# Attention and gated convolution on one core: tables moved among the first steps, routing moved ahead, convolution started later, one broadcast transfer for two, reciprocals of the last pair by PE transposes, more PSUM banks at both ends

## The chip, the core and the metric

The kernel runs on one core of a Trainium2 chip. The metric is the device time of one execution in microseconds (us). Runs of one kernel agree within about 2%. A run more than 1.5% above the fastest of its kernel counts as slow. Ratios and intervals below use fast runs alone; the medians quoted are over all runs. Engines in the profile: PE is TensorE (matrix multiply), PEld its weight loads, DVE is VectorE, ACT is ScalarE, POOL is GpSimd, SP issues most of the transfers (DMA).

## The reference

```python
# attention: B=4, H=8, S=768, D=64, 16 centroids per head
q_assign = argmax(einsum('bhsd,hcd->bhsc', q_n, c_n))      # k_assign likewise
mask     = q_assign[..., :, None] == k_assign[..., None, :]
attn     = softmax(where(mask, q @ k.T / 8, -1e9))
x        = (attn @ v), heads joined to 512 columns
# gated long convolution
x1, x2, x3 = split(x @ w_proj)
y   = x1 * irfft(rfft(x2) * rfft(filter_fft)) * x3
out = y @ w_out
```

## The kernel before

The work goes through 8 groups of four heads (two per batch). A group has 12 attention steps: two pairs of heads, six key blocks each. A step multiplies scores for the next key block, takes their exponent on ACT, multiplies by v ("value matmuls") and adds up the row sums on DVE. Between the matmuls of a step, units of other work are emitted so that PE has something to do: **routing** of the next group (transposes of q and k, similarity to the centroids, a one-hot of the best centroid, whose rows go by DMA into the operands of the scores), and the **convolution** of the batch before, done with matmuls against tables of sines and cosines. PE executes in the order in which the program emits. So does every other engine in its own order, which a scheduler chooses.

```python
def bank():                                   # the PSUM bank of a unit: two take turns
    return psF.tile([128, 512], F32, name="pf")

def routing(n):                               # a generator; each yield ends a unit
    ...                                       # 8 units of transposes, 2 of similarity
    nc.vector.tensor_tensor(oh, cf, m2..., op=Alu.is_equal)          # one-hot, on DVE
    for _ in range(3):
        yield                                 # three empty units
    for t in range(NT):
        nc.tensor.transpose(oT[:, t*128:(t+1)*128], ohf[...], identb) # PE waits for oh here
    nc.vector.tensor_scalar(ohT, oT[:, :S], mka, mkb, ...)
    ...                                       # 8 DMAs of one-hot rows into the score operands

def finish(self):                             # divide a pair's output by its row sums
    ...                                       # sums by 4 matmuls -> den
    nc.sync.dma_start(dd, den[0:128:32])      # through DRAM into another shape ...
    nc.sync.dma_start(dn, dd...)
    nc.vector.reciprocal(dn, dn)
    nc.sync.dma_start(dr..., dn)              # ... and back
    for hp in range(2):                       # broadcast: one row to 64 partitions, twice
        nc.sync.dma_start(rb[64*hp:64*hp+64], dr[hp:hp+1].to_broadcast([64, S]))
    nc.vector.scalar_tensor_tensor(xf, self.osb[:, :S], ..., rb, op0=Alu.add, op1=Alu.mult)
    ...                                       # sums and differences uT, copy xT

# the loop over 96 steps (w = step within the group)
if w == 0:
    for f in fill: drain(f[0])                # what is left of the convolution, in one lump
    fill = [[routing(n + 1), 17, 17], ...]    # routing spread over the twelve steps
if w == 3 and second batch or later:          # convolution of the batch before
    fill.append([hyena(b), 21, 21])
```

Before the loop the kernel routes group 0 and builds all tables; after it, the last pair is finished and the last convolution runs alone.

The softmax here doesn't subtract the row's maximum and nothing guards it: scores larger than these inputs give would overflow.

## Time and profile before

571.07 us (two runs, 568.28 and 573.85). From its profile:

| stage | us from the start |
|---|---|
| first scores / first value matmuls | 53.8 / 56.7 |
| groups 1, 2, 4, 6, 7 start | 93.3, 131.4, 261.1, 392.1, 482.7 |
| last value matmuls end; last convolution; end | 508; 520.7 to 571.7 |

A group "starts" where its first value matmuls start in the trace. Groups 2 and 3, and 4 and 5, are one full period (a batch of attention, one convolution).

The head of the page: busy time of PE, then PE's busy tenths and its granted clock in 40 equal slices.

```profile
span 571.7 us, 6805 instructions
PE 432.3 (76%) x2405; PEld 179.9 (31%) x2417; DVE 339.7 (59%) x459; ACT 257.6 (45%) x432; POOL 177.1 (31%) x168
PE   5015997987689669977689768969689778965675
PEclk9657999989699899989699899998799897996998
```

PE is the busiest engine, with holes, and the clock dips near the holes. The period of groups 4 and 5 in the window view (stretch, its length, busy us of each engine with instruction counts, granted clock, share of the DMA engines, GB/s):

```profile
261.10:392.10 131.00, 105.68 (x593) 43.68 (x592) 79.15 (x104) 61.92 (x105) 43.26 (x30) 0.92 0.24 64
```

PE is busy 105.68 of 131.00 us. What ended its idle time in the period from 130.6 to 259.8 (engine and its work, what it waited for, us in total, times, longest):

```profile
PE pf L391 <- DVE uT L379: 8.0, 1, 8.0
PE ps L325 <- DMA aug_137<-ohT: 3.7, 1, 3.7
PE ps L325 <- DMA aug_145<-ohT: 2.4, 1, 2.4
PE pf L447 <- POOL hy L437: 2.2, 1, 2.2
```

The first line is the convolution's first unit waiting for the last pair of the batch to be finished; the next two are scores waiting for one-hot rows.

```profile
DMA packets 160, 0.39 MB, mean 98 GB/s; under 512 B 32, under 2 KB 32, under 8 KB 160
rb<-dr SPq DMA_DIRECT2D x2, 192.0 KB
```

### The profile page before, as it was taken

What the parts mean: (1) busy time and instruction counts of PE and PEld (TensorE: products, weight loads), DVE (VectorE), ACT (ScalarE), POOL (GpSimd) and SP (SyncE); (2) the same over time, 40 slices, a digit from 0 to 9 for tenths busy, and PEclk for the clock granted to TensorE, in tenths of its full rate; (3) what the DMA queues carried; (4) which work ended last, traced back from release to release, by engine and by line L of the source; (5) the groups of instructions that cost most, each with busy time, mean ns of one, the idle gap of its engine ahead of it and who ended that gap; (6) DMA issues with size and microseconds to landing.
All of it is one profiled execution on the core that took longest, in us unless ns stands there. A gap on an engine that the chain in (4) does not pass through costs nothing.

```text
span 571.7 us, 6805 instructions
## 1 busy us (share of the span) xinstructions
PE 432.3 (76%) x2405; PEld 179.9 (31%) x2417; DVE 339.7 (59%) x459; ACT 257.6 (45%) x432; POOL 177.1 (31%) x168
## 2 busy tenths in 40 slices
PE   5015997987689669977689768969689778965675
PEld 3012433323234224423234224324233233322331
DVE  2907886986369534796269533696368631872630
ACT  4131766746344327746344326736354324742122
POOL 9400704405060133425060233516251221000621
PEclk9657999989699899989699899998799897996998
DMA  8970405315010205315011115312000002010002
GB/s 207 227 165 6 112 20 135 85 42 141 28 29 29 60 10 166 85 43 141 28 29 30 31 39 163 88 37 63 28 1 29 15 1 112 29 31 28 1 1 110
DMA packets 67538, 37.48 MB, mean 66 GB/s; under 512 B 56944, under 2 KB 62640, under 8 KB 67504
## 3 DMA queue, kind: packets, MB, share of 16 engines
q1 hardware_dynamic: 66304, 34.91, 22.4%
q0 software_dynamic: 1056, 2.10, 2.0%
q8 instruction: 19, 0.31, 0.2%
q14 instruction: 15, 0.12, 0.1%
q10 hardware_dynamic: 144, 0.03, 0.0%
HBM read 31.06 MB, written 6.49 MB: 66 GB/s over the span
## 4 chain that ended last, share of the span: by engine, by line
PE 45%; DVE 25%; DMA 10%; issue 8%; SPq 5%; ACT 5%; POOL 2%; POOLq 0%; DVEq 0%; ACTq 0%
PE o L340 15%; PE ps L325 8%; PE pf L391 5%; PE pf L447 4%; DMA rb<-dr 4%; PE pf L412 3%; DVE tm L401 3%; SPq L308 3%; PE pf L262 2%; PE pf L275 2%; PE pf L359 2%; DMA dr<-dn 2%; PE pf L428 2%; DVE uT L380 2%; DMA fhi<-in_moe_filter_fft_dram 1%
## 5 line engine op out<-in xcount | busy, mean ns | idle before, releaser
L329 ACT ACTIVATE p_160<-ps 128x768 f32<-128x768 f32 x32 | 26.0, 812 | 76.1 <-PE ps L325 71.0
L412 PE MATMUL pf<-xT,wpj 128*128 128x384 bf16 x256 | 50.7, 326 | 12.7 <-ACT od L431 5.7
L340 PE MATMUL o<-p_165,vraw 128*64 128x385 f32 (+1 forms) x128 | 55.0, 558 | 0.0
L340 PE MATMUL o<-p_164,vraw 128*64 128x385 f32 (+1 forms) x128 | 55.0, 558 | 0.0
L391 PE MATMUL pf<-wpj,uT 128*128 128x512 bf16 x92 | 30.4, 476 | 32.4 <-DVE uT L379 32.1
L340 PE MATMUL o<-p_161,vraw 128*64 128x385 f32 (+1 forms) x128 | 48.2, 499 | 0.0
L340 PE MATMUL o<-p_163,vraw 128*64 128x385 f32 (+1 forms) x128 | 48.2, 499 | 0.0
L340 PE MATMUL o<-p_160,vraw 128*64 128x385 f32 (+1 forms) x128 | 48.2, 499 | 0.0
L340 PE MATMUL o<-p_162,vraw 128*64 128x385 f32 (+1 forms) x128 | 48.2, 499 | 0.0
L404 POOL TENSOR_TENSOR hy<-tm 128x512 bf16<-128x512 f32 x24 | 32.1, 1360 | 50.1 <-DVE tm L401 50.1
L401 DVE TENSOR_TENSOR tm<-pf,hm 128x512 f32<-128x512 f32 x48 | 30.0, 682 | 18.4 <-PE pf L240 11.3
L329 ACT ACTIVATE p_164<-ps 128x768 f32<-128x768 f32 x32 | 26.0, 812 | 31.9 <-PE ps L325 31.9
L412 PEld LDWEIGHTS <-wpj 128*128 128x128 bf16 x256 | 23.6, 97 | 40.6 <-issue 21.1
L447 PE MATMUL pf<-wout,hy 128*128 128x512 bf16 x92 | 26.4, 438 | 11.4 <-POOL hy L437 8.8
L393 ACT CAST hy<-pf 128x512 bf16<-128x512 f32 x24 | 14.1, 586 | 44.8 <-PE pf L391 44.7
L262 PE MATMUL pf<-ident,qkraw 128*128 128x128 f32 x192 | 33.0, 286 | 1.0 <-ACT qkT L264 0.8
L264 ACT COPY qkT<-pf 128x384 f32<-128x384 f32 x64 | 30.9, 486 | 4.8 <-PE pf L262 4.8
L329 ACT ACTIVATE p_162<-ps 128x768 f32<-128x768 f32 x32 | 26.2, 818 | 14.1 <-PE ps L325 14.1
L262 PEld LDWEIGHTS pf<-ident,qkraw 128*128 128x128 f32 x192 | 25.4, 147 | 8.3 <-ACT qkT L264 2.8
L428 PE MATMUL pf<-inv,hy 128*128 128x384 bf16 (+1 forms) x128 | 22.0, 326 | 7.2 <-DVE x_1550 L417 0.6
L329 ACT ACTIVATE p_163<-ps 128x768 f32<-128x768 f32 x32 | 26.4, 824 | 1.8 <-PE ps L325 1.4
L329 ACT ACTIVATE p_161<-ps 128x768 f32<-128x768 f32 x32 | 26.1, 816 | 0.6 <-PE ps L325 0.2
(477 smaller groups left out, 951.9 us busy)
## 6 DMA issues: line engine op xcount, KB each, us to landing
qkraw<-in_q_dram SPq DMA_DIRECT2D x32, 192.0 KB
qkraw<-in_k_dram SPq DMA_DIRECT2D x32, 192.0 KB
vraw<-in_v_dram SPq DMA_DIRECT2D x8, 768.0 KB
rb<-dr SPq DMA_DIRECT2D x32, 192.0 KB
out_dram<-tm SPq DMA_DIRECT2D x12, 512.0 KB
wpj<-in_moe_w_proj_dram POOLq DMA_DIRECT2D x1, 1536.0 KB, 11.7
flo<-in_moe_filter_fft_dram SPq DMA_DIRECT2D x2, 384.0 KB
fhi<-in_moe_filter_fft_dram SPq DMA_DIRECT2D x2, 384.0 KB
```

The source lines that it names most:

```text
L262: nc.tensor.transpose(tps[:, ts(t, 128)], qr[:, 3 * ch + t].rearrange("p h d -> p (h d)"), ident)
L264: nc.scalar.copy(qkT[z][:, ch], tps[:, :384])
L308: nc.sync.dma_start(augs[aset][pr][hp][j][64 - 16 * hp:80 - 16 * hp], ohT[r0:r0 + 16])
L325: nc.tensor.matmul(sps[:, ch, :384], self.aug[hp][1][:K, ts(sk, 128)], self.aug[hp][0][:K, ts(ch, 384)], start=True, stop=True)
L329: nc.scalar.activation(p[:, :S].rearrange("p (a b) -> p a b", a=2), sps[:, :, :384], Act.Exp, scale=0.125)
L340: nc.tensor.matmul(self.o[64 * hp:64 * hp + 64, ch, :384 + ch], vv[:, 2 * self.pr + hp, sk * D:(sk + 1) * D], pb[hp][sk][:, 384 * ch:384 * ...
L391: nc.tensor.matmul(ps, uvf[:, e, kt, ts(m, 128)], wpj[:, kt, DM:2 * DM], start=(kt == 0), stop=(kt == ND - 1))
L401: nc.vector.tensor_tensor(tm[r][:, cs], ps, hm[:, i, 2 * r + cs], op=Alu.mult)
L404: nc.gpsimd.tensor_tensor(y[:, i, r], tm[r][:, 0], tm[r][:, 1], op=Alu.add)
L412: nc.tensor.matmul(ps[:, :384], wpj[:, kt, off + dt * 128:off + dt * 128 + 128], xT[:, kt, ts(ch, 384)], start=(kt == 0), stop=(kt == ND - 1))
L428: nc.tensor.matmul((pe, po)[e][:, :384], y[lo:hi, i, cs, ts(dt, 128)], inv[lo:hi, row], start=(n == 0), stop=(n == 3))
L447: nc.tensor.matmul(ps, y2[:, kt, ts(2 * tt + e, 128)], wout[:, kt], start=(kt == 0), stop=(kt == ND - 1))
```

## The change

The intent: start attention earlier by building the tables among its first steps; let routing end by step 7, so that one-hot rows are there when the next group needs them; start the convolution two steps later and spread it over both groups instead of draining it; in the last pair replace the DRAM trip by PE transposes, hidden by eight convolution units; let the units at both ends (the first routing, the last convolution) use the banks of the scores too. The core of the diff (layout changes, load order and renamed buffers cut):

```diff
 def bank():
-    return psF.tile([128, 512], F32, name="pf")
+    if spare:
+        return spare.pop(0)
+    if more_banks[0]:                          # at both ends only
+        more_banks[0] += 1
+        if more_banks[0] % 4 in (0, 2):
+            w = psS.tile([128, 2, 512], F32, name="ps")
+            spare.append(w[:, 1])              # the two halves of one tile
+            return w[:, 0]
+    return psF.tile([128, 512], F32, name="pf")[:]
 ...
 def finish(self):
-    for hp in range(2):
-        nc.sync.dma_start(rb[64 * hp:64 * hp + 64], dr[hp:hp + 1].to_broadcast([64, S]))
+    nc.sync.dma_start(rb, dr[:].unsqueeze(1).to_broadcast([2, 64, S]))
+def finish_on_pe(self):                        # last pair: transposes, no DRAM
+    ...
 def hyena(b, xT, uT, last=False):
+    if last:                                   # gates early, then all inversions
+        gates(0); convolve(); gates(1..3); invert(0..3)
 ...
 def emit(nf):
-    (take from the list that is furthest behind)
+    for f in fill:                             # first list with something left
+        if f[1] > 0: f[1] -= 1; next(f[0], None); break
 ...
 if w == 0:
-    for f in fill: drain(f[0])
-    fill.append([routing(n + 1), NR, NR])
+    if n == 0: fill.append([tables(), NTAB, 12])
+    fill.append([routing(n + 1), NR, 7])
+    if hq: fill.append([hq, rest of its units, 12])
-if w == 3 and ...:
+if w == 5 and ...:
     (start the convolution)
```

## The prediction

> **What bounds the kernel now.** TensorE and its waits. The page gives PE 432 of 572 us busy (DVE 340, ACT 258). In the timeline a bare attention step repeats every 2.20 us with PE nearly full, and takes 2.86 with two routing units (2.20 + 2 x 0.33): steps are PE-bound. The chain of waits and PE's wait table show the rest:
>
> - Start: first scores at 53.8 us. PE waits 13.7 us for the one-hot and 14.5 for the filter sum, whose load ends at 44.7; then tables run alone.
> - Each batch period (130.6 to 259.8, three times): 8.0 us for uT at the first convolution unit, 3.7 and 2.4 for one-hot rows at group ends, some 10 of short waits, mostly where the convolution's rest is drained in one lump (196.5 to 219, two banks). After the long waits matmuls take 0.85 instead of 0.49 us, costing about 7 us more; the clock row dips there. The Trainium skill ("TensorE: Matmul & The Clock Gate", "HAM oscillation") warns of PE-idle gaps over about 3.4 us; the trace agrees. About 97 of 129 us is work.
> - End: last values near 510; PE idle 10.7 us until 520.7 (reciprocals through DRAM), then 51 us of the last convolution, with about 14 us of PE waits.
>
> **What changes, stage by stage.**
> 1. Tables move into group 0's first steps. Before first scores some 6.3 MB must load (q, k, v of two groups, filter): at the 210 to 225 GB/s of the window table, about 29 us; the one-hot chain on DVE shares it with sine work and filter sums. First scores near 39 us (34 to 44). The first steps give back 6 to 9 us: about 10 us of DVE evacuations (0.75 each). Group 0 ends at 80 instead of 91: 11 us gained.
> 2. Routing in steps 0 to 6: one-hot rows land before the group ends; 6 us of waits and 4 of slow clock per batch go. Convolution starts later, so the 8 us wait falls below 1.5, with its 2.6 us of slow clock. No lump: about 6 us of its waits hide behind attention. Added: dense steps of five units waiting for evacuations. A batch takes 104 us instead of 129. Group 1 gains 4, two batches 50; group 6 takes 52 instead of 91, as half its convolution moves into group 7: 39.
> 3. The last group now carries units: 26.4 + 1.3 + about 10 + waits = 41 instead of 30: 11 lost. Eight remaining units hide the reciprocals: 9 us instead of 10.7.
> 4. Six banks in the last convolution, gates early, adds and products split between DVE and POOL: PE work about 30 us, then last products and store: 40 instead of 51.
>
> Stage ends: 80, 116, 220, 324, 376, 417, 426, 466. I shade it to 470.
>
> **Predicted: 470 us**, 80% range 452 to 490. Faster by over 2%: 0.96; within: 0.02; slower: 0.02.
>
> **What would show it.** (1) First scores at 34 to 44; first three steps 4 to 5.5 us each. (2) Waits for one-hot rows gone from PE's table, uT waits under 5 us in total, batch period 100 to 108, granted clock in the middle at least 0.96 (now 0.90 to 0.97), PE busy 84 to 88%. (3) Last group about 41 us, no DRAM reciprocals at the end. (4) First projection to end about 40.
>
> **What would make it wrong.** Filter loads ahead of k, or filter sums ahead of the one-hot chain on DVE, delaying first scores past 45. Fill units stalling in-order PE on DVE or ACT evacuations, since DVE goes to about 75% busy: a batch near 112, giving 490. The uT chain slowed by q and k loads on the same queue. Less stall than I charge: 452.

## More of the kernel before

The broadcast of the reciprocals, which will matter: first the chain that ended last (start, us, what), then the DMA view of the 4 us around it, then what DVE waited for at the instructions that read rb (us, times).

```profile
140.49 1.50 DMA dr<-dn
142.55 3.29 DMA rb<-dr
145.96 1.03 DVE x_1165 L377
```

```profile
DMA rb<-dr: 28.2, 9
```

128 packets carry the rows (3072 bytes each). The 32 packets under 512 B are of 4 bytes, 16 for each of the two transfers. I read them as completion marks, one from each DMA engine that took part.

## The result, and the profile after

**650.44 us** (two runs, 651.56 and 649.32), 13.9% slower: the ratio is 1.139, 95% interval 1.114 to 1.164. (A ratio is the mean time of one kernel's fast runs over that of the other's in the same rounds, so it is not quite the ratio of the medians quoted.) I had expected 470.

The head of the page after, with the shares of the chain that ended last:

```profile
span 649.7 us, 6805 instructions
PE 455.3 (70%) x2426; PEld 184.8 (28%) x2426; DVE 341.5 (53%) x474; ACT 259.3 (40%) x430; POOL 151.4 (23%) x154
PE   1538899089249587779785885789667688958565
PEclk9959899689759697799999798889879699779798
PE 42%; DMA 23%; DVE 19%; issue 6%; ACT 6%; POOL 1%; SPq 1%; DVEq 0%; ACTq 0%; POOLq 0%
DMA rb<-dr 19%; PE o L347 15%; PE ps L332 7%; PE pf L460 5%; PE pf L499 3%; DMA dr<-dn 2%; PE pf L366 2%; PE pf L478 2%; DVE tm L447 2%; DMA vraw<-in_v_dram 1%; PE ps L460 1%; PE pf L436 1%; POOL hy L487 1%; DVE uT L420 1%; ACT qkT L273 1%
```

The costliest item of the chain is now a transfer of 384 KB, 19% of it; as two transfers it was 4% before. One landing in the chain, the DMA view of the ten us around it, and DVE's wait in total:

```profile
250.08 9.36 DMA rb<-dr
```

```profile
DMA packets 130, 0.39 MB, mean 39 GB/s; under 512 B 2, under 2 KB 2, under 8 KB 130
rb<-dr SPq DMA_DIRECT2D x1, 384.0 KB
```

```profile
DMA rb<-dr: 107.7, 15
```

The same 128 data packets, but two completion packets instead of 32: two DMA engines carried it. A second view agrees. The busy tenths of the 16 DMA engines, in 40 slices of the same two windows, before and after, stay at 1 while the one transfer runs (two of 16 engines are 12.5%), and reach 8 and 9 for the two:

```profile
DMA  0000000000466974877787876211000000000000
DMA  0000001011111111111111111111111111110000
```

In the chains it takes 9.4 to 12.5 us instead of 3.3 to 5.6. The Trainium skill states the rule in "DMA: Bandwidth & Descriptors", section "Rules for kernel authors": an outermost dimension of size c below 16, such as a leading broadcast, confines the DMA to at most c engines. The source here is walked as 2 x 64 x 768, and the trace agrees: two.

DVE executes in order, and what stands behind the read of rb waits too. The timeline of DVE at that landing (start, us, instruction, and in brackets the idle time before it and what ended it; two lines of uT are left out before the last):

```profile
252.57 0.96 DVE L304 TENSOR_TENSOR oh<-cand,m_1724 128x768 bf16<-128x768 bf16 x1
259.53 1.02 DVE L387 SCALAR_TENSOR_TENSOR x_1636<-osb,rb 128x768 f32<-128x768 f32 x1 [6.01 <-DMA rb<-dr]
260.47 0.67 DVE L312 TENSOR_SCALAR ohT<-pf,mka,mkb 128x768 bf16<-128x768 bf16 x1
262.31 0.95 DVE L354 TENSOR_TENSOR acc_1643<-acc_1643,p_144 128x768 f32<-128x768 f32 x1
```

Routing's evacuation (ohT) and the row sums (acc) stand behind data that they do not use: PE had finished the input of ohT at 254.4, and ohT starts at 260.47. In PE's waits this shows under other names:

```profile
PE pf L310 <- DVE oh L304: 64.8, 7, 20.9
PE pf L249 <- DVE tm L447: 19.8, 3, 9.8
```

The waits of the kernel before are gone: none for uT, and one of 5.5 us for one-hot rows, at the very start. The period of groups 4 and 5 runs from 308.9 to 454.6, 145.7 us, instead of 131.

### The profile page after: what moved, and what is told of

Read it like the earlier page. It is cut to its first block, busy times and chain, and to the rows that moved or that the text cites. A ratio compares the mean times of both kernels' runs of the same rounds, so it can differ in the third digit from the quotient of the medians.

```text
span 649.7 us, 6805 instructions
## 1 busy us (share of the span) xinstructions
PE 455.3 (70%) x2426; PEld 184.8 (28%) x2426; DVE 341.5 (53%) x474; ACT 259.3 (40%) x430; POOL 151.4 (23%) x154
## 3 DMA queue, kind: packets, MB, share of 16 engines
q10 hardware_dynamic: 3968, 2.36, 1.5%
## 4 chain that ended last, share of the span: by engine, by line
PE 42%; DMA 23%; DVE 19%; issue 6%; ACT 6%; POOL 1%; SPq 1%; DVEq 0%; ACTq 0%; POOLq 0%
DMA rb<-dr 19%; PE o L347 15%; PE ps L332 7%; PE pf L460 5%; PE pf L499 3%; DMA dr<-dn 2%; PE pf L366 2%; PE pf L478 2%; DVE tm L447 2%; DMA vraw<-in_v_dram 1%; PE ps L460 1%; PE pf L436 1%; POOL hy L487 1%; DVE uT L420 1%; ACT qkT L273 1%
## 5 line engine op out<-in xcount | busy, mean ns | idle before, releaser
L347 PE MATMUL o<-p_141,vraw 128*64 128x385 f32 (+1 forms) x128 | 58.1, 584 | 0.0
L347 PE MATMUL o<-p_142,vraw 128*64 128x385 f32 (+1 forms) x128 | 58.1, 584 | 0.0
L336 ACT ACTIVATE p_144<-ps 128x768 f32<-128x768 f32 x32 | 26.3, 822 | 76.7 <-PE ps L332 75.9
L460 PE MATMUL pf<-xT,wpj 128*128 128x384 bf16 x212 | 46.4, 351 | 9.8 <-DVE tm L447 6.6
L347 PE MATMUL o<-p_146,vraw 128*64 128x385 f32 (+1 forms) x128 | 52.1, 533 | 0.0
L347 PE MATMUL o<-p_145,vraw 128*64 128x385 f32 (+1 forms) x128 | 52.1, 533 | 0.0
L310 PE MATMUL pf<-identb,oh 128*128 128x128 bf16 x42 | 5.1, 283 | 64.8 <-DVE oh L304 64.8
L347 PE MATMUL o<-p_144,vraw 128*64 128x385 f32 (+1 forms) x128 | 48.9, 506 | 0.0
L347 PE MATMUL o<-p_143,vraw 128*64 128x385 f32 (+1 forms) x128 | 48.9, 505 | 0.0
L336 ACT ACTIVATE p_145<-ps 128x768 f32<-128x768 f32 x32 | 25.9, 810 | 54.9 <-PE ps L332 54.9
L336 ACT ACTIVATE p_141<-ps 128x768 f32<-128x768 f32 x32 | 25.9, 811 | 41.9 <-PE ps L332 37.1
L450 POOL TENSOR_TENSOR hy<-tm 128x512 bf16<-128x512 f32 x21 | 28.1, 1353 | 51.1 <-DVE tm L447 31.7
L336 ACT ACTIVATE p_142<-ps 128x768 f32<-128x768 f32 x32 | 26.1, 815 | 29.6 <-PE ps L332 27.4
L336 ACT ACTIVATE p_143<-ps 128x768 f32<-128x768 f32 x32 | 26.2, 819 | 24.3 <-PE ps L332 24.1
L278 POOL CAST aug_138<-qkT 64x768 bf16<-64x768 f32 x16 | 15.8, 988 | 79.4 <-ACT qkT L273 78.8
L499 PE MATMUL pf<-wout,hy 128*128 128x512 bf16 x80 | 23.8, 426 | 13.5 <-DVE yy L486 6.9
L271 PE MATMUL pf<-ident,qkraw 128*128 128x128 f32 x174 | 27.3, 284 | 7.8 <-ACT qkT L273 7.5
L332 PE MATMUL ps<-aug_136 80*128 80x384 bf16 x96 | 24.6, 339 | 6.4 <-DMA aug_136<-ohT 5.5
L336 ACT ACTIVATE p_146<-ps 128x768 f32<-128x768 f32 x32 | 26.1, 817 | 6.7 <-PE ps L332 5.4
L478 PE MATMUL pf<-inv,hy 128*128 128x384 bf16 (+1 forms) x108 | 21.5, 358 | 10.2 <-DVE ohT L312 5.1
L332 PE MATMUL ps<-aug_137 128*128 128x384 bf16 x96 | 26.3, 359 | 2.2 <-ACT p_141 L336 2.2
```

Of the source, the lines that this page charges most:

```text
L271: nc.tensor.transpose(tps[:, ts(t, 128)], qr[:, 3 * ch + t].rearrange("p h d -> p (h d)"), ident)
L278: (nc.gpsimd if n else nc.vector).tensor_copy(augs[aset][0][:D, z], qf[:D])
L332: nc.tensor.matmul(sps[:, ch, :384], self.aug[hp][:K, 2 * self.pr + 1, ts(sk, 128)], self.aug[hp][:K, 2 * self.pr, ts(ch, 384)], start=Tru ...
L336: nc.scalar.activation(p[:, :S].rearrange("p (a b) -> p a b", a=2), sps[:, :, :384], Act.Exp, scale=0.125)
L347: nc.tensor.matmul(self.o[64 * hp:64 * hp + 64, ch, :384 + ch], vv[:, 2 * self.pr + hp, sk * D:(sk + 1) * D], pb[hp][sk][:, 384 * ch:384 * ...
L450: (nc.vector if last and r else nc.gpsimd).tensor_tensor(y[:, i, r], tm[r][:, 0], tm[r][:, 1], op=Alu.add)
```

## The experiments

**Theory A**: the single transfer uses two DMA engines, lands 6 to 7 us later, and in-order DVE passes the delay on. **Theory B**, the rival: routing pulled ahead puts the one-hot chain behind the row sums on DVE, however long the transfer takes; rb is merely where DVE is seen waiting. The kernels of one call ran on the same chip; e1, e2, e3 and e6 were one call, e4, e7, e8 and e9 a second, e10 to e12 a third, e13 a fourth. Across calls I compare ratios to the kernel before, which had medians of 574.55, 571.78, 571.46 and 573.65 us in them.

### e1: two transfers again

```diff
-nc.sync.dma_start(rb, dr[:].unsqueeze(1).to_broadcast([2, 64, S]))
+for hp in range(2):
+    nc.sync.dma_start(rb[64 * hp:64 * hp + 64], dr[hp:hp + 1].to_broadcast([64, S]))
```

> The changed kernel with one thing undone: the reciprocals are broadcast to 128 partitions by two transfers of 64 partitions, as before the change, instead of one. Theory A (the single transfer with an outermost size of 2 is carried by 2 of 16 DMA engines, lands in about 10 us instead of 3.3, and VectorE, which runs in order, stands still behind it): the wait of DVE for rb falls from 107.7 us to under 30, TensorE's wait for the one-hot from 71 us to under 15, and the time lands at 465 to 505 us. Theory B (routing pulled ahead puts the one-hot chain behind the attention adds on in-order VectorE, whatever the transfer takes): the time stays above 560 us.

560.9 us, ratio 0.981 (0.971 to 0.990). The transfer was worth 90 us, and DVE no longer waits for rb at all. The other two marks of theory A were missed: PE's wait for the one-hot fell from 71.4 to 33.7 us (27.1 among the steps, 6.6 at the start), not below 15, and 561 is not 465 to 505. By its total alone the run meets theory B's mark (above 560), so e1 does not decide between the two as causes of the loss; e2 does. The other 91 us of my error lie elsewhere, and the wait at the one-hot, to which theory B points, is among them.

### e2: the kernel before with the one transfer

> The kernel before, with one thing of the change added: the one broadcast transfer in place of two. Theory A: each of 16 landings takes about 10 us instead of 3.3; 6.7 us more, of which the schedule hides part: 630 to 680 us. Theory B: the kernel before has its routing late and hides it, under 595 us.

The edit of e1 reversed, on the kernel before: 660.6 us, ratio 1.152 (1.143 to 1.162). DVE's wait for rb:

```profile
DMA rb<-dr: 120.5, 16
```

One line of the change, alone, costs 15% under the old schedule, where routing is late. Theory B, which expected under 595, falls as the cause of the loss, and theory A stands.

### e3: one transfer, outermost size 64 (wrong result on purpose)

```diff
-nc.sync.dma_start(rb, dr[:].unsqueeze(1).to_broadcast([2, 64, S]))
+nc.sync.dma_start(rb, dr[:].unsqueeze(0).to_broadcast([64, 2, S]))
```

> The changed kernel, still one broadcast transfer of the same bytes, but with the source walked so that its outermost size is 64 and the two heads come inside; partitions then get the wrong head's reciprocals, so the result is wrong on purpose. Theory A (engines are given out by the outermost size): lands in 3 to 4 us with 32 completion packets instead of 2 and 128 data packets as before, and the time equals that of the two-transfer kernel within 1.5%. If what costs is one large transfer as such: 10 us and about 650 us again.

The DMA view of one landing, and the landing times (the trace gives them for four of the fifteen):

```profile
DMA packets 144, 0.39 MB, mean 94 GB/s; under 512 B 16, under 2 KB 16, under 8 KB 144
rb<-dr SPq DMA_DIRECT2D x1, 384.0 KB, 3.3
```

```profile
DMA to landing us min/median/max: 3.2/3.2/5.0
```

Still one transfer of the same bytes, now on 16 engines, and it lands in 3.2 to 5.0 us. (I had expected 32 completion packets; 16 is right for one transfer.) So what costs is not that it is one, but how its outermost dimension is cut. The time is 571.6 us (two runs), 1.9% over e1, a little more than the 1.5% I had allowed. Its trace shows part of why: DVE waits 10.8 us for rb in nine places (in e1 in none), and group 1 takes 43.9 instead of 38.1 us, with 6.3 instead of 2.9 us of waiting for the one-hot and a granted clock of 0.92 instead of 1.00. The rest is left open.

### Where the other 90 us went: e1's trace

The stage ends of e1 contradict the prediction. (The trace is of e1's longest run, 566.03 us; its other three took 560.4 to 560.9.)

| stage end | predicted | e1 | before |
|---|---|---|---|
| group 0 | 80 | 96.8 | 93.3 |
| group 1 | 116 | 134.9 | 131.4 |
| group 3 | 220 | 264.1 | 261.1 |
| group 5 | 324 | 393.7 | 392.1 |
| group 6 | 376 | 458.8 | 482.7 |
| last value matmuls | 417 | 492 | 508 |
| last pair finished | 426 | 502.5 | 520.7 |
| end | 466 | 564.0 | 571.7 |

The differences between prediction and e1, stage by stage, are 16.8 (group 0), 2.1 (group 1), 50.8 (two periods), 13.1 (group 6), -7.7 (last group), 1.4 (last pair) and 21.5 (last convolution): 98.0 us in all. A period takes 129.6 us in this trace, not 104:

```profile
264.10:393.70 129.60, 108.34 (x598) 44.19 (x594) 77.44 (x104) 62.45 (x104) 36.90 (x31) 0.92 0.23 64
```

PE's longest waits in it:

```profile
PE pf L310 <- DVE oh L304: 8.2, 2, 4.1
PE pf L249 <- DVE tm L448: 4.0, 2, 3.2
PE pf L500 <- POOL hy L488: 2.9, 1, 2.9
```

The old waits (uT, one-hot rows, the lump) have gone, and new ones of nearly the same size have come. The one-hot is the clearest. Routing may now take up to five units in a step, so its three empty units, meant to give DVE time, pass within one step, and PE reaches the transposes while DVE still works. The PE timeline of e1 there (idle before it, and its releaser, in brackets):

```profile
402.29 1.51 PE L347 MATMUL o<-p,vraw 128*64 128x384 f32 x8
403.74 0.50 PE L332 MATMUL ps<-aug 80*128 80x384 bf16 x2
408.98 0.82 PE L310 MATMUL pf<-identb,oh 128*128 128x128 bf16 x6 [4.74 <-DVE oh L304]
410.37 2.83 PE L347 MATMUL o<-p,vraw 128*64 128x384 f32 x8
413.89 1.51 PE L347 MATMUL o<-p,vraw 128*64 128x384 f32 x8
```

After 4.74 us of idleness the eight value matmuls take 2.83 us instead of 1.51: PE's clock has dropped (0.55 granted from 407 to 413.8). The Trainium skill ("TensorE: Matmul & The Clock Gate", section "HAM oscillation") puts the rule at PE-idle gaps above about 3.4 us; this gap is above it. But it is no safe limit here: in the kernel before, gaps of 2.51 us (to 124.72) and 2.36 us (to 192.48) were followed by a clock of 0.50 too. Such a gap is paid twice.

### e7: nine empty units instead of three

```diff
-        for _ in range(3):
+        for _ in range(9):
             yield
-NR, NH, NTAB = 17, 43, 13
+NR, NH, NTAB = 23, 43, 13
-                fill.append([routing(n + 1), NR, 7])
+                fill.append([routing(n + 1), NR, 10])
```

> On the kernel with two transfers (560.9 us): nine empty units instead of three between the start of the one-hot on VectorE and the PE transposes of it, in every routing. Its trace shows TensorE standing 4 to 5 us at these transposes in every group (27 us in all) and matmuls at 0.86 instead of 0.50 us in the step after, because up to five units a step use up the three empty ones within one step. Theory C (this new wait is what ate the gain in the middle): the wait falls below 6 us, about 40 us with the slow clock come back in part, 520 to 540 us. Rival (VectorE's queue is behind anyway and the wait moves to the next reader): above 552 us.

549.35 us, ratio 0.962 (0.955 to 0.969); the intervals of e1 and e7 do not overlap. The period of groups 4 and 5 falls to 123.2 us, from 129.6 (126.3 and 126.4 in the traces of e4 and e9, which share the middle of e1). The wait among the steps falls from 27.1 to 12.1 us, not below 6, and another grows: the output projection waits 3.9 to 4.2 us for its product on POOL instead of 2.9. Both readings were partly right: 549 lies between the two expectations. (The edit also spreads routing over ten steps instead of seven; which of the two helped was not tried.)

### e6: tables before the steps again

```diff
+    drain(tables())                 # after routing(0), as in the kernel before
     ...
-    if n == 0: fill.append([tables(), NTAB, 12])
```

> Two transfers, and the tables built before the attention steps again instead of among the first ones. If moving the tables gains what I predicted (about 7 to 11 us), this is 5 to 12 us slower than the two-transfer kernel; if the first steps only pay later for what the start gains, within 3 us.

556.0 us, ratio 0.970 (0.957 to 0.983), against 0.981 for e1. I had expected this to be slower by 5 to 12 us. The total alone would be unclear, but the stage shows it: the first value matmuls start at 53.2 instead of 49.0 us, and yet group 0 ends at 90.5 instead of 96.8. Among the steps the tables cost more than they save before them: the first three steps of e1 take 7.0, 5.5 and 4.1 us, those of e6 4.9, 4.0 and 3.4. (The traces of e4, e8 and e9, which have the same start as e1, end group 0 at 93.9 to 96.9.)

### e4, e8, e9: the last convolution

From the last value matmuls to the end e1 takes 71.9 us, with 61.5 from the first projection; the kernel before took 63.5 and 51. (Traces of e3, e6 and e7, whose last convolution is that of e1, take 69.2 to 73.2 for this stretch, so differences of some 4 us say nothing.) The PE timeline of e1 at those projections:

```profile
502.49 1.03 PE L437 MATMUL ps<-wpj,uT 128*128 128x512 bf16 x4
504.19 1.02 PE L437 MATMUL ps<-wpj,uT 128*128 128x512 bf16 x4 [0.67 <-ACT hy L439]
505.05 1.03 PE L437 MATMUL pf<-wpj,uT 128*128 128x512 bf16 x4
505.91 1.03 PE L437 MATMUL ps<-wpj,uT 128*128 128x512 bf16 x4
507.61 1.02 PE L437 MATMUL ps<-wpj,uT 128*128 128x512 bf16 x4 [0.67 <-ACT hy L439]
```

Whenever two ps units follow each other, the second waits until ACT has copied the first: they are the halves of one tile, and the wait goes by tile, not by half. So a pair may be worse than two banks in turn. (**Theory D**.)

e4 uses the two ordinary banks in the last convolution (the line that turns on further banks there is removed):

> On the kernel with two transfers: no more PSUM banks for the last convolution (the two of the rest of the kernel). If six banks help as I predicted, 3 to 8 us slower than 560.9. Theory D (two banks are halves of one tile, and the trace shows the second half's matmul waiting 0.7 us for the copy out of the first, so that they add little): within 3 us.

551.6 us, ratio 0.966 (0.959 to 0.974). From the last value matmuls to the end: 63.2 us. Six banks were 8.7 us slower than two; I had expected a gain from six, or at most no difference.

e8 takes one half of each pair and leaves the other unused:

```diff
-        if more_banks[0] % 4 in (0, 2):
-            w = psS.tile([128, 2, 512], F32, name="ps")
-            spare.append(w[:, 1])
-            return w[:, 0]
+        if more_banks[0] % 2 == 0:
+            return psS.tile([128, 2, 512], F32, name="ps")[:, 0]
```

> On the kernel with two transfers: at both ends each further bank is the first half of a tile of its own, so four banks, none sharing a tile, instead of six of which four share two tiles. Theory D: the 0.7 us waits of TensorE at every third unit disappear, 3 to 8 us faster than 560.9. If the number of banks counts: slower by some us.

549.1 us, ratio 0.959 (0.949 to 0.968), and 57.5 us from the last value matmuls to the end. The same projections in e8's PE timeline follow each other without a wait:

```profile
502.21 1.03 PE L435 MATMUL ps<-wpj,uT 128*128 128x512 bf16 x4
503.07 1.03 PE L435 MATMUL pf<-wpj,uT 128*128 128x512 bf16 x4
503.94 1.03 PE L435 MATMUL ps<-wpj,uT 128*128 128x512 bf16 x4
```

Four banks that share no tile beat six of which four share tiles (71.9), by more than the 3 to 8 us I expected, and theory D holds. Of the 14.4 us, 9.0 are gaps (25.2 to 16.2) and 5.4 busy time, as the clock is 0.91 instead of 0.85; waits at second halves are only a part of these gaps. Whether four such banks beat two (63.2) is less sure: the totals of e4 and e8 do not differ clear of noise, and only 1.8 of the 5.7 us are gaps.

e9 keeps the six banks and runs the last convolution in the old order (`last=True` removed from the call):

> On the kernel with two transfers: the last convolution in the old order (each inversion after its own gates, products on POOL), with the further banks kept. The trace of the two-transfer kernel shows 61 us from the first projection to the end, the kernel before 51. If the new order costs, because four inversions run back to back over one intermediate tile (TensorE waits 4.4 us there), this is 5 to 11 us faster than 560.9; if the order helps and something else costs, slower.

554.0 us, ratio 0.970 (0.964 to 0.977), 65.0 us from the last value matmuls to the end. The old end is some 7 us shorter with these banks, but the cause that I expected is not shown. `last=True` sets not only the order, but also which engine does the adds, products and last copies. Of the 6.9 us only 2.3 are gaps; the rest is busy time, at a clock of 0.94 instead of 0.85. And in e8, which keeps the new order and changes the banks, the wait of 4.4 us that I had in mind is down to 1.7.

### e12: everything mended, old schedule

e8 and e6 together, with the old emission, the old starts and the lump.

> The kernel of two transfers, banks that share no tile and tables first, but with the schedule of the kernel before: routing spread over twelve steps, convolution from step 3, its rest drained in one lump. Theory E (moving routing ahead and spreading the convolution gained next to nothing in the middle, because waits of about the same size came back in other places: 130 us per batch in both traces): batch period 128 to 131 us, and a total of 550 to 562 us, of which the gain on 571 comes from the end. If the old schedule is what held the kernel before back: over 565.

558.8 us, ratio 0.980 (0.974 to 0.985); groups 4 and 5 take 129.7 us, with 21.6 us of waits for uT and 17.9 for one-hot rows over the whole run. **Theory E** holds: the new schedule, as written, gained little in the middle. Two periods take 257.8 us in e12, and 252.8 to 258.8 in the traces of e1, e4, e8 and e9, which share their middle; 50 us of gain were foretold. It did gain in the last two groups: 98.4 us in e1, 112.2 in e12, 116.2 before.

### e10 and e11: mended versions

e10 is e6, e7 and e8 together:

> The three repairs that each helped the two-transfer kernel (560.9 us), together: nine empty units before the one-hot transposes, further banks that share no tile, tables before the attention steps. Alone they gave about 11, 12 to 14 and 5 us. If they act in different stages they add: 528 to 538 us. If one only works because the others are absent: above 540.

523.75 us, ratio 0.917 (0.911 to 0.922). The repairs add up; that it is below the 528 expected is not clear of the noise in the three gains.

e11 goes on with what was left in the middle:

```diff
-        for _ in range(3): yield                      # routing's empty units
+        for _ in range(10): yield 'idle'
-                    next(f[0], None)
-                    break
+                    if next(f[0], None) != 'idle':    # an empty unit lets another unit run
+                        break
-            if hq:
+            if hq and g == 1:                         # do not spend units on a finished convolution
-        if w == 5 and g == 0 and n > 0:
+        if w == 6 and g == 0 and n > 0:
+        for _ in range(3): yield 'idle'               # before the output projection
         yield from expand()
 # last convolution: gates(0), convolve, then gates(dt), invert(dt - 1) in turn
```

> As the combined kernel, and units of the convolution run while routing is in its empty units; the convolution of a batch starts with 21 units over six steps rather than 20 over four; three empty units before the output projection; in the last convolution each inversion follows the gates of the next block. Its target is the waits left in the middle, some 17 us per batch with 4 us of slow clock, and 4.4 us at the end. 505 to 525 us if the waits vanish; above 528 if they only move.

**498.1 us**, ratio 0.872 (0.868 to 0.877), correct: the fastest kernel here, and below the 505 I expected at best. Its period of groups 4 and 5:

```profile
242.30:352.60 110.30, 99.31 (x596) 42.14 (x592) 78.61 (x104) 62.01 (x105) 36.64 (x30) 1.00 0.29 77
```

and PE's longest waits in that period:

```profile
PE pf L477 <- DVE x L464: 3.6, 4, 2.2
PE pf L269 <- ACT qkT L271: 2.5, 4, 1.0
PE pf L247 <- DVE tm L446: 1.2, 1, 1.2
```

The clock does not fall here: it is 1.00, and the same instructions keep PE busy for 99.31 us instead of 108.34. That is partly luck. The gap of 2.2 us at L477 comes once in each of the three convolutions among the steps; in groups 2 and 3 (112.8 us, clock 0.97) and in group 6 the clock fell after it. This splits e1's 129.6 us: 99 of work, about 9 of slow clock (108.3 - 99.3), 21 of gaps (129.6 - 108.3). e11 has 11 us of gaps. The edits of e11 were not tried one by one.

### e13: the slow transfer in the best schedule

> The fastest kernel so far (498.1 us) with the one broadcast transfer put back. It asks whether a schedule with more slack hides a 10 us landing. If VectorE's in-order queue stands still behind each of 15 landings whatever the schedule (theory A): 6.7 us more each, 60 to 100 us slower, 560 to 600 us. If the slack hides it: under 530 us.

The edit of e2, on e11: 593.5 us, ratio 1.041 (1.031 to 1.051), 95 us slower than e11. DVE's wait for rb:

```profile
DMA rb<-dr: 96.8, 15
```

The three schedules lose 86 (before), 90 (changed) and 95 us (e11) to the same line, about 6 us for each of the 15 or 16 landings. No schedule here hides it: DVE stands at all 15 reads of rb, 96.8 us in total. A schedule that puts other DVE work ahead of these reads was not tried.

## Why the prediction was wrong

It had the sign wrong: 470 foretold, 650 measured. The error of 180 us has two halves.

- **The term that is missing: the broadcast.** The diff shows it, and step 3 and the risks speak of the reciprocals, but the prediction gave the new form of the transfer no cost. It assumed, without saying so, that one transfer of the same bytes takes the same time. 90 us (e1), against 6.7 us of extra landing each. The page of the skill that states the rule was at hand and was not used for this line.
- **Step 1, tables among the first steps.** First scores came at 40.4 us, inside 34 to 44. But "the first steps give back 6 to 9 us" was undersized: the first values came 8.0 us after the first scores in e1 (2.9 before), the first steps took 7.0, 5.5 and 4.1 us, slow clock included, and group 0 took 47.8 us from its first values (36.6 before) and ended at 96.8, not 80. Building the tables first is better (e6).
- **Step 2, the middle.** "A batch takes 104 us": 129.6 in e1. The mechanism was right in its first half: the waits for uT and for one-hot rows did go, with the lump. The step that failed is the charge for "dense steps of five units waiting for evacuations": 104 less 97 of work leaves some 7 us for all waits and slow clock, and e1 had 21 of gaps and about 9 of slow clock. The same change that let routing end early used up routing's empty units, so PE waited for the one-hot itself, 4 us a group plus the slow clock, and for products on POOL and DVE. The kernel before had 25 us of gaps in this period. The estimate of work was right: 97 us said, 99.3 in e11.
- **Steps 2 and 3, last groups and last pair.** 33.3 us for the last group (458.8 to 492.1) instead of 41, but 65.1 for group 6 instead of 52: together 98.4 instead of 93, so the sum was nearly right and its split was not. 10.4 us to finish instead of 9.
- **Step 4, the last convolution.** "40 instead of 51": 61.5 in e1. "Six banks" was the step that failed: four of them are halves of two tiles, and with independent banks alone the stretch after the last value matmuls lost 14.4 us (e8). "PE work about 30 us" was 39.0 us of busy time, at a clock of 0.83.
- **What would show it.** PE busy 84 to 88% and a middle clock of at least 0.96 were foretold: 70% and 0.84 to 0.89 after (0.92 in e1). e11 reaches 84%, with 0.97 and 1.00 in its two periods. These marks described the kernel that the change intended, not the one it was.

What stays open: how much of e11's gain over e10 each edit gives, what of `last=True` costs in e9, and most of the 1.9% between e3 and e1.

## What to carry to other kernels

Count the completion packets of every new transfer: the outermost dimension of its source, not its bytes, set its time here, and an in-order engine passed a 6 us delay on to everything queued behind it. When work is moved ahead to remove a wait, ask which slack that work relied on; a wait that leaves one place tends to come back at the next dependency, so judge a new schedule by the sum of gaps and the clock of a period rather than by the wait that was aimed at. Buffers that are halves of one tile can be worse than fewer plain ones (six banks with two such pairs against two: 71.9 and 63.2 us here).

## What the Trainium skill lacked or had wrong

- "DMA: Bandwidth & Descriptors", section "Rules for kernel authors", was right (outermost size 2: two completion packets, 9.4 to 12.5 us; 64: 16 and 3.2 to 5.0 us). It lacks how to read the number of engines off a profile: next to 128 data packets of 3072 bytes stood 2, 16 or (two transfers) 32 packets of 4 bytes.
- "TensorE: Matmul & The Clock Gate", section "HAM oscillation", gives about 3.4 us as the gap to avoid. In e11 the same gap of 2.23 us came three times; the next eight value matmuls then took 2.83, 1.51 and 2.69 us. In the kernel before, a gap of 2.51 us was followed by a clock of 0.50. So a single shorter gap can cost, but does not always.
- "PSUM — Partial Sum Buffer" has nothing on a two-bank tile used as two buffers: matmuls into its second half waited 0.67 us for the copy out of its first, and six banks, four of them such halves, were 8.7 us slower than two plain ones.
- No page that I read puts a number on an in-order VectorE behind a late transfer: about 6 us lost for each landing that came 6 to 7 us later, in three schedules.
